# Attention with a routed expert layer on one core: the order of work on the engines made again with other costs of TensorE

## The chip, the cores and the metric

The kernel runs on one core of one Trainium2 chip. The metric is device time in microseconds (us), the median of several runs. The core has five engines that work side by side, each through its own instructions in a fixed order: TensorE (PE, matrix products; its loading of weights is shown apart, as PEld), VectorE (DVE), ScalarE (ACT), GpSimd (POOL), and SyncE (SP), which here issues transfers alone.

## The reference, cut to what matters

```python
# q, k, v: 8 batches x 8 heads x 576 positions x 64, float32
q_rot, k_rot = rotate(q), rotate(k)                      # rotary tables of 576 positions
scores = 1 / np.sqrt(64) * q_rot @ k_rot.transpose(0, 1, 3, 2)
attn = np.exp(scores - scores.max(-1, keepdims=True))
attn = attn / (attn.sum(-1, keepdims=True) + 1e-9)
x = (attn @ v).transpose(0, 2, 1, 3).reshape(8, 576, 512)
out = x.copy()
for b in range(8):
    s = x[b] @ w_gate
    top = np.argpartition(-s, 128)[:128]                 # 128 rows of the 576
    y = np.maximum(x[b, top] @ w1, 0) @ w2               # 512 -> 1024 -> 512
    out[b, top] = x[b, top] + y / (1 + np.exp(-s[top]))[:, None]
```

## The kernel before

The attention goes in 16 groups, g0 to g15, of four heads each (two groups make a batch). A group has two pairs of heads, c0 and c1. Pair number 2g + c of q and k is loaded by SP's transfers and multiplied with the rotary tables (`rotate`), nearly always on POOL: for q and for k a product of 128x1152 and a sum of 128x576, and for q a transfer `q_in<-q_in` behind them, which carries the result across partitions. Only the first pairs give some of these sums and products to DVE.

`units` is the product of 64 queries of a group with all 576 keys, for one pair or both: matmuls `banks<-k_in,q_in`, eight tiles of the array at a time (32 rows by 64 columns each; g0 uses four tiles of 64x64). `softmax` then takes the scores out of the PSUM banks in one of two ways, which the letters of `DRAINS` choose for each pair and block of queries:

- V: one DVE instruction, TENSOR_SCALAR_CACHE_REDUCE `prob<-banks`, scales, copies and finds the minimum.
- S: ACT copies (ACTIVATE `prob<-banks`), and DVE finds the minimum in a second instruction (TENSOR_REDUCE `nm<-prob`).

ACT then does the exponential (ACTIVATE `prob<-prob,nm`, 288 in all), and DVE transposes 32x32 blocks (`turn`). `value` is the product with v, again eight tiles (`banks<-prob,vt`, six parts of 48 matmuls a group); its result is copied (`ot<-banks`), transposed on PE (`banks<-ident,ot`) and scaled by ACT or DVE (`x<-banks,rs`). POOL multiplies the rows with the gate (`prod<-x,wg`), ACT or DVE adds them up, and each batch is routed: ranks, choice, an indirect load of 128 rows, the two products with w1 and w2 (whole-array matmuls), and an indirect store.

What stands in which order on each engine is decided nowhere in the loops. Each piece of work is recorded as an operation (`Order.op`), and `LINES` lists, engine by engine, the numbers of all operations in the order in which they are issued, two characters each. An operation that can go on two engines goes to the one in whose line it stands. `Order.run` walks through these lines with costs written in the code and gives out the PSUM banks by the times it gets; these costs are also those with which the lines were made. For PE it counts a change between kinds of tiles (`SWITCH`), a beginning after a wait, and a supply time: PE's instructions come in blocks of `BLOCK` = 256, and a block is not entered earlier than `FETCH` ns after the one before. Eight PSUM banks are shared: a pair's block of scores takes two, `value` takes banks 0 to 3, all other products one.

Of the kernel before, what the change touches and what calls it, by code (L numbers as in the profile page):

```python
# [33 lines left out]
fAhsfBfChxfDfEcyfNisfLfJiFizhHiMhIhJhKiRhLhMiXj7j1hRgbhThVcCcDkIkDgicFcGjdkOkZkUl3glcIcJcKcLjol9jpjqlejrjsjtlkmfjyjAjCgo
mrmEmlmylulvmLlwlxmQlylzmVm-lGlEgsgtopoBovk0lIgvgwoUoIoOo+k7gygzgAgBpap4nanbkancndnenfqdq6nonmkdnkplpmqqpnqkpoqCppqwpqkh
qInOpvpxpzkiqOshqUnVkkklsnstknkonYsykpkqr2sFr3sMr4r5sYr6r7sSn-rgrerct2tSu8tYu2o3o4o6rGueo7urultduxtetfuDtgthtirNo9tntrtp
oarQuRuSuTuUuVuWrTobv3v1u-ocrXverYr+vls1vor-s2s3vrs4vvvwvyvBvzvCvDvE""",
# [2 lines left out]
3N5i2a28263I3L3S5D3P2f5N5w5r5W5o5k5G5t5y5B5I5L5V5-5Y5m5q5S615Q41406X2h7647726-79492j7f6W744e7q717u4g7H6Z7h4i7D7b7s7A787k  # L40
7p7m7e7F7y7C7w6d6e7J7L6i95989c9f9m9j6m979o6r9q9h9e4V9a9u9l9z9H9s6t9L7Y7X9B9J9P9F9W9D9x829O4Z9UaOb29R8ba-8daXaU50b1b9b6bj
bdaQbbb8bhaWb4aZbsbnblaSbqa6a7bzbxbfd2bvd8bDdfdbbBaddhdldjdoafd6dddaakdsd4d08Ic+amdudndqdwdBaobPbQdzdGdKbY8HdEeEeRdJdMeK
eNeId+eVc3eXeMePeGf3eZeTe-f9f8f2dYdZc5fbfefge5f5e1fiflea8PgSfpgWecfkfngQftfrgVgYh0h7fHh4eecAhhhbhlg-hph2h9h6hjhfhuhohrhd
hwhzfGfFfOcziwhBitiGiJfTiCiyiviBiEiQfXiOiLiIiShNhOi+jaj2iWj0hShWiZiUkJh-jcj4j6i1j9cHjgkRl0i3jfkFjikHkNkWl4kLjwl8l2kYgqkQ
kTlbk-lfl6lhldljjvjulmmglojDgpmsmvmFmImmjImBjKmqmkmimomKmPmAmDmumxmHlBlAjMmYmSn0mNlHmXm+gumUoqoCoFlJoun2own4gxoXoJoRoHoE
lOoyoAoWosoQoZlQo-pdoNpcoTp7p3p1oLpfp9p6ngnhqeqhlSqaq7kennqjqtq9qcqvqlqgqpqDkfqzqsprqHqFqLpyqykjqPsiqnqKqTqRqNqBkmsopFqW
sqqYpHsksssCszsvrasmsxo1sGsJsEpJsBsNsIsLsPsZsRr9r8sTt1o0rhsVt3sXtTt7u9t5rms-tZrotVrqo5tXu3udubuiufo8u5usuot-u7uuu1uAuhuk
uwunuCuquHuztjtkuFtstxrVrUtzv2tBvtvA""",
# [2 lines left out]
323w3B3D3T3c3U3K3O5l3R5K3H5j5M5C5A5x5v5H5F3V435s5U5+605X5R5P635p6462666V6Y6545737d706g7o7j7a7l7r7x7g7K7I7v774F7M4I7E4J4L
4K4M7B7O4O7P6k7Q7N969n4R9g9k9t7+999d9r9y9w4W9X9K9I9Y9E9C9N9V4U9T846v9Q809ZaR899-9+8sb0aP8z8y8v8x8waVbmb7a9bgbab3aYbrbpbe
bkbFbwbubEbCc-cZd58BabbHbAdcdidgbIbGdmd98EbSdp55d3dOdvdtdNdAdydPdFdDdIbUbWdLeHc1dQdReU8MeLeOeFe+eYeSd-f1fuf78Jfvfaf4fdff
ckgRgPcne3cpcrcocqfwfjctfmfsgUg+gXfqfxfyhCcw8UcBhkh8fIhehch1hnh5hihqhthvhDhyhAhEhFfMfKhGiAiuhQixiKiPiDiHfViNjjiVjkiTiYi-
j8gajbgfghgegdj3gghUj5cEkMjlgjkKkGkEjekPk+kVl1gmjhl7jmkSjnl5kXjxcMlplalcgrlqlglilrlllnmjjzjBltlsmpmtmwmzmJmnmhmGmOmMmCn5
mRmTn6j-mWn3lDlFmZn1n7otn8k5k3k4oGozk6k2oDoVnjoMoxoPp2oSk8oroKn9oYpggCpbp5k9p0p8pekbpipkpjphqiqfnlnpq8qbnupuqrquqonwqmny
qGqZkgqAqxnNpsqEqJnUnSpwpAnQnRnTqMqSqQslqVqXnWq+r0spsusrsjswq-sDnZr1krrbsAt8sKo2sQsHsOt9t0s+tasWsUrfrdt6t4tWuctUu0uatctb
u6rFt+uIrMrIrLrJu4rKujuvtmumutuLuguyupuKuBuEuJuGuNuOrOuPuMuQtotqrRuYrWu+uXv4v9v0v6v7v8v5vdodvgvkvivhvjrZvmvnvps0vsvxs5vu
vF""",
# [1 line left out]
0z0E0A0B0H2L2M2N2O2I2J2G2H575859235e5a5f5c5d2e6R426S6M6N6P2g6K6L6Q6f2i8Y4d8Z4f914h8W8X924H8-904PaK7Z6qaL4S6saFaGaIaD6uaJ
aE888a8ca8cV8ucWcQcRcTcUcOcP8CeAbRevajeweyaleBezan8Feteu56c0c2gLgEgMgGgHgFgJgKc4cme9ebcuiiedijipiqcxikiliniofShPkAfUkBfW
8Vkvkwkykzktkugch+i0i2gkmcgnmdmam7m8mbm5m6lCjHohjJcNoiomonofjLokogolq1lNp+niq3lPq4p-k1pYgDpZkcq2lRs9saptsentnvnxsfscs7sd
nPs8pEnXtIpGtPtJtQtKkspIn+tNtOtLrlrnrptlrHrPuZrStwtytAvfoevqs6vG""",
# [3 lines left out]
at8raqapcXcS6o6naCcccdcac9aAc8cb85ayaz87c6ceexaB86c7cheCcfagemelefegeiehcgekb-cjciejgNgIahenesaib+bZg5eoe7fZg2fYf+erg3f-
g1e6e8epeqirg0g4imiai8ibg8idg6g7g9i7i4i6i9fQkCfPi5iekxifihjVicfRhZhXjTjRjUjOjShYjQjNjPjWmeigm9jYjXlWlZlVj+l+lXjZlUlTlYm2
ojl-jGoojFnDnEnznBnFnCm1m4nGjEnHlLnInAm3lMlKm0q0pMq5pNpQpPpRnKnJpKpLpTnMpOnLpSpXpUpWnspVsbsgrznqrArsryrrrxrunrpDrtrvrwtR  # L70
pCrDtMrErCripBtCrBrjtErktGtHtFtDvctuttvavbtv""",
}


# [240 lines left out]
def attention_moe_kernel(ctx: ExitStack, tc: tile.TileContext, q, k, v, w_gate, w1, w2, rope, halves, outs, cap):  # L315
# [156 lines left out]
    DRAINS = (
        ("SVVSVVSSS", "SSSVSSSVS"),
        ("SSSVVSVSS", "SSSSSVVSS"),
        ("SSVVVVVVV", "VSVVVVVSV"),
        ("VSSVVVSSS", "SSSSVSVSV"),
        ("SSSSVSSVV", "SSSVVVVSV"),
        ("SSSSSSVVS", "VSSSVVVVV"),
        ("VSSSSSVVV", "VVSVSVVVS"),
        ("SSSSVVVSS", "VSVVSSVSV"),  # L480
        ("VVVSSSVVV", "VSSSVVSVV"),
        ("SVSVSVSVV", "SSSVVSVSS"),
        ("VSVVVSVSV", "VVSVSVVVV"),
        ("SSSVSVVVS", "VVSSSVVSV"),
        ("SSSSVVSVV", "VVSVSSVSS"),
        ("SSSVVSVSV", "SSVSSVSVV"),
        ("SSVSSSSSS", "VVVSSVVVV"),
        ("SSSSSVSVV", "VVVVSSVSV"),
    )
# [630 lines left out]
```

## Time and profile before

| | |
|---|---|
| median of 3 runs | 511.87 us (511.4 to 513.64) |
| the profiled execution | 514.22 us, of it 512.5 us in the span of its records |
| PE busy | 481.9 us, 10148 matmuls and as many weight loads |
| DVE busy | 448.5 us |
| ACT busy | 393.4 us |
| POOL busy | 351.0 us |
| moved by DMA | 86.86 MB, mean 169 GB/s |

Busy time is the sum of the instructions of an engine over the whole span. The start differs from the rest: in the first 125 us PE is busy for 107 us, and from 125 us to 446 us for 313.9 of 321 us.

### The profile page before, as it was taken

To read this page: it belongs to the slowest core of one execution; us is meant where nothing else is said; L and a number is where in the kernel's file an instruction comes from. 1 tells how busy PE (TensorE), PEld (TensorE's weight loads), DVE (VectorE), ACT (ScalarE), POOL (GpSimd) and SP (SyncE) were. 2 spreads that over 40 slices of the span, in tenths; PEclk is the share of its full clock that TensorE was granted. 3 is DMA by queue.
4 is the path that set the end of the run, shared out by engine and by line. 5 is a ranking of instruction groups with operands and counts; after the bars stand their busy time and mean duration, and the time that the engine had idled before them with its cause. 6 is when DMAs were issued, how large, how long until landed. Compare 5 with 4: busy or idle time off the path is not lost.

```text
span 512.5 us, 23466 instructions
## 1 busy us (share of the span) xinstructions
PE 481.9 (94%) x10148; PEld 343.0 (67%) x10148; DVE 448.5 (88%) x783; ACT 393.4 (77%) x1065; POOL 351.0 (68%) x316
## 2 busy tenths in 40 slices
...
GB/s 286 287 228 256 200 206 181 228 172 199 220 194 155 179 180 222 157 183 195 187 208 134 184 153 185 161 229 141 214 138 186 190 103 128 24 86 23 114 22 41
DMA packets 52488, 86.86 MB, mean 169 GB/s; under 512 B 5920, under 2 KB 29216, under 8 KB 52384
## 3 DMA queue, kind: packets, MB, share of 16 engines
...
q8 instruction: 80, 1.31, 1.1%
q10 hardware_dynamic: 544, 0.59, 0.4%
q14 instruction: 24, 0.20, 0.1%
...
## 4 chain that ended last, share of the span: by engine, by line
PE 71%; ACT 8%; POOL 8%; issue 6%; DMA 3%; DVE 3%; SPq 0%; POOLq 0%; DVEq 0%
PE banks L241 71%; ACT prob L241 5%; POOL k_in L241 4%; POOL q_in L241 3%; DMA q_in<-q_dram 2%; ACT ot L241 2%; DVE prob L241 2%; ACT x L241 1%; POOL prod L241 1%; DMA k_in<-k_dram 1%; ACT prod L241 0%; SPq L241 0%; POOL out_dram L241 0%; DVE q_in L241 0%; POOLq L1115 0%
## 5 line engine op out<-in xcount | busy, mean ns | idle before, releaser
L241 ACT ACTIVATE prob<-prob,nm 128x576 f32<-128x576 f32 x288 | 220.7, 774 | 20.3 <-DVE prob L241 14.1
L241 PE MATMUL banks<-k_in,q_in 32*64 32x288 f32 (+1 forms) x4464 | 191.0, 415 | 19.8 <-ACT prob L241 6.2
L241 DVE STREAM_TRANSPOSE prob<-prob 128x2304 f32<-128x2304 f32 (+2 forms) x98 | 186.5, 1923 | 0.5 <-ACT prob L241 0.3
L241 PE MATMUL banks<-prob,vt 32*64 32x288 f32 x4608 | 163.3, 404 | 1.8 <-issue 0.6
L241 PEld LDWEIGHTS banks<-k_in,q_in 32*64 32x64 f32 (+1 forms) x4464 | 109.1, 133 | 79.7 <-ACT prob L241 19.1
L241 PEld LDWEIGHTS banks<-prob,vt 32*64 32x64 f32 x4608 | 120.7, 132 | 33.2 <-issue 7.6
L241 DVE TENSOR_SCALAR_CACHE_REDUCE prob<-banks 128x576 f32<-128x576 f32 x140 | 102.8, 748 | 19.3 <-PE banks L241 18.0
L241 ACT ACTIVATE prob<-banks 128x576 f32<-128x576 f32 x148 | 93.1, 652 | 29.8 <-PE banks L241 29.3
L241 DVE TENSOR_REDUCE nm<-prob 128x1 f32<-128x576 f32 x148 | 105.7, 737 | 1.1 <-ACT prob L241 1.0
L241 POOL TENSOR_TENSOR prod<-x,wg 128x512 f32<-128x512 f32 (+1 forms) x45 | 49.5, 1100 | 56.6 <-ACT prod L241 16.6
L241 POOL TENSOR_TENSOR q_in<-q_in,tabk 128x1152 f32<-128x1152 f32 (+1 forms) x31 | 80.5, 2597 | 7.6 <-DMA q_in<-q_dram 5.4
L241 POOL TENSOR_TENSOR k_in<-k_in,tabh 128x1152 f32<-128x1152 f32 x30 | 79.6, 2657 | 5.5 <-DMA k_in<-k_dram 3.5
L241 PEld LDWEIGHTS banks<-xt,w1t 128*128 128x128 f32 x512 | 58.9, 192 | 4.1 <-issue 3.6
L241 PE MATMUL banks<-xt,w1t 128*128 128x128 f32 x512 | 61.2, 277 | 0.0
L241 PE MATMUL banks<-w2t,ht 128*128 128x512 f32 x128 | 58.5, 599 | 0.0
L241 ACT ACTIVATION_READ_ACCUMULATOR prob<-prob,nm 128x1 f32 x288 | 57.3, 199 | 0.0
L241 POOL TENSOR_TENSOR q_in<-q_in 128x576 f32<-128x576 f32 (+2 forms) x33 | 45.2, 1371 | 10.4 <-DVE q_in L241 9.2
L241 POOL TENSOR_TENSOR k_in<-k_in 128x576 f32<-128x576 f32 x31 | 43.8, 1417 | 2.7 <-DVE k_in L241 1.4
L241 PEld LDWEIGHTS banks<-w2t,ht 128*128 128x128 f32 x128 | 23.0, 190 | 24.4 <-issue 22.9
L241 POOL TENSOR_SCALAR sel<-slots,rank 128x128 bf16<-128x128 bf16 x30 | 17.7, 604 | 26.8 <-DVE rank L241 26.8
L241 ACT ACTIVATE x<-banks,rs 128x64 f32<-128x64 f32 (+1 forms) x144 | 31.2, 322 | 4.5 <-PE banks L241 3.3
L241 ACT ACTIVATE prod<-prod 128x256 f32<-128x256 f32 (+1 forms) x63 | 25.8, 414 | 9.1 <-POOL prod L241 9.1
...
## 6 DMA issues: line engine op xcount, KB each, us to landing
...
```

The source lines that it names most:

```text
L241: i = made(*args, **kwargs)
```

## The change

Two costs of TensorE are raised, and the tables that follow from them are made again. After a wait the beginning of an operation of eight tiles counts 130 ns instead of 70 (the other two kinds stay at 70), and the supply time of a block of instructions counts 3950 ns instead of 3600. `LINES` (all five engines) and `DRAINS` are new. Every operation of the reference is computed as before; no tile, pool or transfer is added or removed.

```diff
-BLOCK, FETCH = 256, 3600.0
+BLOCK, FETCH = 256, 3950.0
+
+
+RESTART = (70.0, 130.0, 70.0)
...
     "PE": """
-010T1r101i190J1H1v1A0O141N0X1e1m3d2V333o2Q3i2+381X3u1Y1Z3A1+1-3F203M5h29275J255z5u5E5T5n5Z5O3W3X3Y3Z3+3-6U7546446+487c7n
+010T1i1q10190J1m0O1z1G0X1M1u1d143a302S3k3f352O2X1V3r1W3y1X1Y3E1Z1+3K5e27235G255w5B5p5k5S5Y5M3T3U3V3W3X3Y6T7441436Z457b7n
...
-                            begin += SWITCH[mode][o.mode] + 70.0 * (t > free[e] + 1)
+                            begin += SWITCH[mode][o.mode] + RESTART[o.mode] * (t > free[e] + 1)
...
     DRAINS = (
-        ("SVVSVVSSS", "SSSVSSSVS"),
-        ("SSSVVSVSS", "SSSSSVVSS"),
-        ("SSVVVVVVV", "VSVVVVVSV"),
+        ("SVVVVVSSV", "SSSSVSSVS"),
+        ("VSSVSSVSV", "SSSVSSSVS"),
+        ("SVSVVSSVV", "VVSVVVVSV"),
```

The letters V in `DRAINS`, group by group from g0: before 6, 5, 14, 7, 8, 8, 10, 8, 11, 8, 13, 7, 9, 8, 8, 10 (140 of 288); now 8, 6, 12, 6, 10, 6, 11, 7, 9, 6, 11, 7, 9, 7, 9, 10 (134).

Of the operations that can go to two engines, the scaling of rows (`x<-banks,rs`) stands in ACT's line 24 times before and 20 now (DVE 24 and 28), adding up the gate's products 38 and 34 times (DVE 7 and 11), the relu of the expert layer (`ht<-banks`) 11 and 15 times (DVE 5 and 1). PE's line has 394 operations before and now, of the same kinds.

The rows below are instructions in the order in which they stand on an engine, equal ones that follow each other in one row. The first place is ACT in g0 and at the beginning of g1, before and then now: `prob_87<-banks` is an S copy of g0, `prob_88<-banks` one of g1, `prob_87,sums_92<-prob_87,nm_94` an exponential of g0.

```order
L241 ACTIVATE prob_87<-banks 128x576
L241 ACTIVATE prob_87,sums_92<-prob_87,nm_94 128x576
L241 ACTIVATE prob_87<-banks 128x576 x4
L241 ACTIVATE prob_87,sums_92<-prob_87,nm_94 128x576
L241 ACTIVATE prob_87<-banks 128x576 x2
L241 ACTIVATE prob_87,sums_92<-prob_87,nm_94 128x576 x3
L241 ACTIVATE prob_87<-banks 128x576
L241 ACTIVATE prob_87,sums_92<-prob_87,nm_94 128x576 x2
L241 ACTIVATE prob_87<-banks 128x576
L241 ACTIVATE prob_87,sums_92<-prob_87,nm_94 128x576 x5
L241 ACTIVATE prob_88<-banks 128x576
L241 ACTIVATE prob_87,sums_92<-prob_87,nm_94 128x576
```

```order
L244 ACTIVATE prob_87<-banks 128x576 x4
L244 ACTIVATE prob_87,sums_92<-prob_87,nm_94 128x576 x4
L244 ACTIVATE prob_87<-banks 128x576 x3
L244 ACTIVATE prob_87,sums_92<-prob_87,nm_94 128x576
L244 ACTIVATE prob_87<-banks 128x576
L244 ACTIVATE prob_87,sums_92<-prob_87,nm_94 128x576 x3
L244 ACTIVATE prob_87<-banks 128x576
L244 ACTIVATE prob_87,sums_92<-prob_87,nm_94 128x576 x5
L244 ACTIVATE prob_88<-banks 128x576 x5
L244 ACTIVATE prob_88,sums_93<-prob_88,nm_95 128x576
```

g0 has two S copies fewer, and the first five copies of g1 now stand together behind the last exponential of g0.

The second place is DVE in g0, behind its first products of the rotation, before and then now: TENSOR_SCALAR `prob_87,nm_94<-banks` is a V, `q_in_75` and `q_in_76` are the queries of the first two pairs.

```order
L241 TENSOR_SCALAR prob_87,nm_94<-banks 128x576 x3
L241 TENSOR_TENSOR q_in_76<-q_in_76,tabk 128x576
L241 STREAM_TRANSPOSE prob_87<-prob_87 128x576 x2
L241 TENSOR_REDUCE nm_94<-prob_87 128x1
L241 STREAM_TRANSPOSE prob_87<-prob_87 128x576
```

```order
L244 TENSOR_SCALAR prob_87,nm_94<-banks 128x576 x3
L244 TENSOR_TENSOR q_in_76<-q_in_76,tabk 128x576
L244 TENSOR_TENSOR q_in_75<-q_in_75 128x192
L244 STREAM_TRANSPOSE prob_87<-prob_87 128x576
L244 TENSOR_SCALAR prob_87,nm_94<-banks 128x576
```

A sum of 192 columns that stood on POOL stands on DVE now, ahead of the first transpose.

The third place is ACT where g1 ends and g2 has its scores taken out, before and then now: `prob_87<-banks` is an S copy of g2 here, `x_90<-banks,rs_96` the scaling of g0's rows.

```order
L241 ACTIVATE x_90<-banks,rs_96 64x64 x4
L241 ACTIVATE x_90<-banks,rs_96 128x64 x16
L241 ACTIVATE prob_88,sums_93<-prob_88,nm_95 128x576 x3
L241 ACTIVATE prob_87,sums_92<-prob_87,nm_94 128x576
L241 ACTIVATE prob_88,sums_93<-prob_88,nm_95 128x576
L241 ACTIVATE prod_98,gp_99<-prod_98 128x256 x2
L241 ACTIVATE prob_87,sums_92<-prob_87,nm_94 128x576 x2
L241 ACTIVATE prob_87<-banks 128x576 x3
L241 ACTIVATE prob_87,sums_92<-prob_87,nm_94 128x576 x15
```

```order
L244 ACTIVATE x_90<-banks,rs_96 128x64 x8
L244 ACTIVATE prob_87<-banks 128x576
L244 ACTIVATE x_90<-banks,rs_96 128x64 x8
L244 ACTIVATE prob_88,sums_93<-prob_88,nm_95 128x576 x3
L244 ACTIVATE prob_87,sums_92<-prob_87,nm_94 128x576
L244 ACTIVATE prob_87<-banks 128x576 x2
L244 ACTIVATE prob_87,sums_92<-prob_87,nm_94 128x576 x2
L244 ACTIVATE prob_87<-banks 128x576
L244 ACTIVATE prod_98,gp_99<-prod_98 128x256 x2
L244 ACTIVATE prob_87,sums_92<-prob_87,nm_94 128x576 x4
L244 ACTIVATE prob_87<-banks 128x576
L244 ACTIVATE prob_87,sums_92<-prob_87,nm_94 128x576 x11
```

g2's S copies are six instead of four, and they stand between the scalings and exponentials rather than in one piece.

## Rows read from the trace of the kernel before

**Rows 1.** Page, busy time of each engine and its share of the span.

```profile
PE 481.9 (94%) x10148; PEld 343.0 (67%) x10148; DVE 448.5 (88%) x783; ACT 393.4 (77%) x1065; POOL 351.0 (68%) x316
```

**Rows 2.** Windows: length, then busy time of each engine, PE's granted clock, DMA.

```profile
0.00:36.00 36.00, 26.61 (x220) 16.54 (x220) 30.92 (x63) 21.59 (x49) 22.56 (x25) 1.00 0.82 266
36.00:60.00 24.00, 23.39 (x598) 17.20 (x606) 23.22 (x36) 20.78 (x49) 17.27 (x13) 0.93 0.78 234
60.00:97.00 37.00, 31.39 (x810) 18.70 (x794) 35.05 (x59) 35.78 (x112) 29.22 (x24) 0.95 0.68 197
97.00:125.00 28.00, 25.54 (x713) 19.18 (x721) 27.28 (x46) 27.14 (x76) 26.01 (x27) 1.00 0.67 201
125.00:446.00 321.00, 313.87 (x6942) 226.11 (x6925) 300.11 (x504) 269.49 (x728) 242.29 (x207) 1.00 0.59 172
446.00:512.50 66.50, 61.14 (x905) 45.22 (x889) 31.96 (x80) 18.64 (x57) 13.69 (x23) 0.99 0.18 55
```

**Rows 3.** Windows, four short stretches of the start, same columns.

```profile
28.00:36.00 8.00, 2.63 (x32) 1.16 (x32) 8.00 (x12) 8.00 (x22) 7.84 (x4) 1.00 0.68 189
36.00:40.00 4.00, 4.00 (x56) 2.33 (x60) 3.68 (x6) 2.23 (x5) 3.92 (x3) 0.58 0.92 287
...
60.00:70.50 10.50, 7.44 (x188) 3.70 (x172) 10.10 (x22) 10.50 (x39) 6.66 (x8) 1.00 0.69 211
70.50:74.50 4.00, 3.86 (x72) 2.37 (x80) 2.90 (x8) 4.00 (x11) 3.92 (x3) 0.57 0.64 153
```

**Rows 4.** Timeline of PE: start, length, matmuls; in brackets PE's idle time before.

```profile
31.70 1.91 PE L241 MATMUL banks<-k_in,q_in 32*64 32x288 f32 x24 [2.95 <-DMA q_in<-q_in]
36.00 7.47 PE L241 MATMUL banks<-k_in,q_in 32*64 32x288 f32 x121 [2.39 <-ACT prob L241]
...
66.54 2.58 PE L241 MATMUL banks<-k_in,q_in 32*64 32x288 f32 x64 [0.33 <-DVE prob L241]
70.64 3.89 PE L241 MATMUL banks<-k_in,q_in 32*64 32x288 f32 x64 [1.52 <-ACT prob L241]
```

**Rows 5.** Chain that ended last, its longest piece: start, length.

```profile
446.40 50.41 PE banks L241 x841
```

**Rows 6.** Groups of ACT: count, busy us, mean ns of one.

```profile
L241 ACT ACTIVATE prob<-banks 128x576 f32<-128x576 f32 x148 | 93.1, 652 | 29.8 <-PE banks L241 29.3
L241 ACT ACTIVATE x<-banks,rs 128x64 f32<-128x64 f32 (+1 forms) x144 | 31.2, 322 | 4.5 <-PE banks L241 3.3 <-POOL sel L241 1.2
L241 ACT ACTIVATE prod<-prod 128x256 f32<-128x256 f32 (+1 forms) x63 | 25.8, 414 | 9.1 <-POOL prod L241 9.1
L241 ACT ACTIVATE ht<-banks 128x512 f32<-128x512 f32 x11 | 6.6, 604 | 16.9 <-PE banks L241 16.8
```

**Rows 7.** Groups of DVE, same columns.

```profile
L241 DVE TENSOR_REDUCE nm<-prob 128x1 f32<-128x576 f32 x148 | 105.7, 737 | 1.1 <-ACT prob L241 1.0
L241 DVE TENSOR_SCALAR_CACHE_REDUCE prob<-banks 128x576 f32<-128x576 f32 x140 | 102.8, 748 | 19.3 <-PE banks L241 18.0 <-ACT prob L241 0.3
L241 DVE TENSOR_TENSOR x<-banks,rs 128x512 f32<-128x512 f32 (+1 forms) x24 | 14.7, 634 | 1.4 <-PE banks L241 1.4
L241 DVE TENSOR_REDUCE gp<-prod 128x2 f32<-128x512 f32 (+1 forms) x7 | 4.2, 606 | 1.1 <-POOL prod L241 1.1
L241 DVE TENSOR_TENSOR k_in<-k_in 128x288 f32<-128x288 f32 x2 | 0.9, 458 | 0.1
```

**Rows 8.** Waits from 125 to 446 us: total, times, longest.

```profile
PEld banks L241 <- ACT prob L241: 16.1, 35, 1.3
```

**Rows 9.** Timeline: weight loads behind a gap; two long runs of eight-tile matmuls.

```profile
47.84 1.21 PEld L241 LDWEIGHTS banks<-prob,vt 32*64 32x64 f32 x48 [0.71 <-issue]
...
307.19 0.91 PEld L241 LDWEIGHTS banks<-prob,vt 32*64 32x64 f32 x33 [0.75 <-issue]
...
452.73 4.60 PE L241 MATMUL banks<-prob,vt 32*64 32x288 f32 x144
```

**Rows 10.** Page, the DMA queue that brings PE's instructions: packets, MB, share.

```profile
q8 instruction: 80, 1.31, 1.1%
```

More of the change, by code (lines that the diff above doesn't have):

```diff
@@ L34 @@
[L34 to L37, printed above, removed]
-    "ACT": """
-0203121t0K0V1a1k1I0M1w1c1B0P151E1K1O0Y1D1M1y1n0R1Q1R1G171T1p1g3e0+2W343r2R3g3l3q2-392T2Y3v363k313n3b3t3z3x3C3E3G3J21223Q
@@ L40 @@
[L40 to L48, printed above, removed]
-    "DVE": """
-0s0t0w0x0u0v0G0y0U0D0C1s111j0F131u0L0W1b1l1L0N1J1d1x0Q161C1F1P1f0Z1V1o0S1z1S1U1W181q1h2X353f3p3s0-3j3m2S3h303a3y2Z372U24
@@ L51 @@
[L51 to L59, printed above, removed]
+010T1i1q10190J1m0O1z1G0X1M1u1d143a302S3k3f352O2X1V3r1W3y1X1Y3E1Z1+3K5e27235G255w5B5p5k5S5Y5M3T3U3V3W3X3Y6T7441436Z457b7n
+7h7u7G7A6667684D696a6b4K6g6i9b949i6k4N7R9o7S9u7T7U9F7V7W9z9K9Q4Q7-81834U4VaLaYaR4X4Y8tb3bgba9+bm9-a0a1bsa2a3bycYd28Aa8df
@@ new lines @@
+d84+aaac8D4-50dl51bJdrbKbLbMdwbNbOdBdGbVbXbT8GeCePeI8K8LdReWdSf0dTdUf6dVdWfcgOe1cld-e38Nfh8OcsfogTgZh38Qcv8R8S8Thghafzhm
+fAhsfBhyfCfDfEcyfNiufLfJiHiBhJiOhKiUhLhMhNhOi+jaj5hVhXhTgbcCcDkHkNcFgicGjhl8kTkZl2glcIcJcKcLjslejtjujvlkjwjxlqmljCjEjGgo
+mxmJmrmElAlBlCmQlDmXlElFn1n6lMlKgsgtovoHoBlOk4gvgwo+oOoUp4kbgygzgAgBpgpangkenhninjnknlqcqjnsnunqkhprqwpsqqptqKpuqDpvpwkl
+nUpBqQkmpFn-pDqVsoq-kokpsvsBkro2kssHktkur9sOrasVrbrct3rdres+rnrlrjo5t8tYufu9u2o9oaocrNuloduyustjuEtktltmuJtntorUoftttxog
+rXtvuXuYuZu+u-v0r+ohv5v7v9s2oivks5s3vrs8vus6s9savxsbvEvBvCvFvHvIvJvK""",
+    "ACT": """
@@ new lines @@
+02030V1s0K1k120M0P1A1D1H1C1F0R1J1v0Y1e1L151O1g1b1P0+171R1o1x3b312T3o3l3d36332V2Y2Q3j3v3s3h3n3q3B3x382+3u3A3D3F1-203N3J5f
+28245H263P3M3H5A5t5q5h5D5V2d5F5y5J5L5N5m5j5s5o5+5v5P5R5U605X3Z3+6W2f787544716+2h6Y7e7o4b7r7i7q4d7v7H704f6V737x7B7m7a7k7z
+7g7t7L7D7d7F6c6d7J776h9c9f95989l6l9a9h9p9k4S979e6q9r9t9n6s9y9J7X7Y9A9w9N9E9H9C9U9M824W9SaMb09PaS8baV8daZaQ4ZaOb7b4bhblbd
+aUb6b9a-b2brbnbfaXbtbcbjbpa5a4bzcZd3bBdgd9bxbDdcbvd1abdkaddodbd7dedid5aic-dndvakdqdtdyamdAbPbQ8IdJdFdD8HeDeTdLdIeMdZeJeQ
+8MeHeLeVeXeOeFf3c3eSe-eZf7f9dYdXf5c5fbf2e0e4fefgflfigS8PfkfpgWfnfte9gVgYgQh0frebh7edg-h4cAhhhbh9hdhphlh2h6hthohjhrhBhfhv
@@ new lines @@
+hxhAfFfGfOcziyhDiviIiLiChRiRiGixiEiTiAiNiViQiKhPhQi-j2fXjbjej1hUj4cEkIiZiXi3kOjgj9cHjdjkl9kWj7jjl5k-i5jml1kMkSkKgqkQlbkY
+l4lhldkVl7lnlgljlmjyjzlplsmmlujHgpmymBmNmKmsjMmqlImumomwmAmUmRmGmDjOmImPm+lGlHmTmMmWlNn5mZn0gun3owoIoLlPoAnan8oCgxp1oPoV
+lUp0oEoyoGoKlWoXp3p9p5pjpboRoZpfp7oToNplpipdkjnnnmqdqgqkqnkiqAqxqmnAqtqpqfqNqiqCqHqEnEqJpyqsqzqPqMqvknpGqUqWssspq+pLqSqY
+kqsrswr1sEr3qGrhpNsLsAsIsDsysKo7susGsSsPsNsZsXsUsRt7rgrfrot5o6t9t0tZrtugt2tdu3rvu6tbucuirxobu1t-u5umupuboeukuzuvuxu8ueuo
+uBuuuruGuDuNuLtptquItuv3s0v2tFr-tHv6s4vzs7vG""",
+    "DVE": """
@@ new lines @@
+0s0t0w0x0u0v0G0y0U0D0C1j1r110F0B0W1a0L1t1n130N0Q1B1E1I1K1N1S0S1l1f1w160Z1T1Q1h0-1c1U1p18323c221y3i3g2U372P343m3p3e3w2W3t
+3z2R2Z3C3Q3I3R3O3G5i393L2-5K5I5g5z5x5C5E3S5n5l5r5T5-405Z5u5W5Q5O636162656U64466X42767c6f796-7p7l7f727y7K7s7j7w4C7I7M7E4J
+4G4I4H7C4F7O4L7P6j7Q7N994O9j9g969s9q9m9d9x9v9V9G9I4T7+9W9D9B9L9T4R9R809X846u9OaP899Z9Y8saNa+8y8z8w8x8vaTbkbibbb5a7b8beb1
+bqaWbFbobwbubEbCbAd0c+d68Ba9d4bGdhdjdabHbIdm8EbSdddp52dNdudsdMdxdzdOdCdEdHbWbYbUdKeGc18JdPdQeEeNeKeUe+eYeRf1fud+f4faf8fv
+fffdckgPgRcqe2cpcrcncofwfjctfmfsgUg+fqgXfxcwhEfy8Uhkh8hecBhch1hnh5hihqhwfIhFhuhzhGhHhCfMfKhIiFiwiDhSfTiPiziSiJfViMiYjnjo
@@ new lines @@
+iWgaj0j8j6hYgfj3hWgeggghgdjci1jfkJkLjpgjkRkPjilckUk+l3jll0jqkXgmjrlacMl6grlvlflwjBlilllxlolrltmpjDjFlylzmvmtmnmCmLmFmHmz
+mOnblJmVmYmSncn4n2n7n9m-lLndjQozk3nekak8k6k9oFoJk7oMo-oSoDoxoYnfoWp8oQp2kcpmgCphnpkdp6pepopkkfpcpnpqppntnrnvlYqeqhqoqlqB
+qyqrqLqOnCpAr4qInTkkqFpxqunXn+nZnWqRnYpCqTpEo0qZr5r0qXr2sqr7sCszstsxo3r6r8sJsFkvrisMtesTsQsYsWtft4t6tgt1o8s-rmrkpPtctau0
+ujt+uauhthu4tirMudu7rQrTuOrRrPrSuquCutuwuRuntsuAuPuHuFuTuQuMuKuSrVuWuUuVtwv4tyrYtDs1v1v8vdvavevfvcvbvjojvqvmvnvpvovsvtvv
+vyvDvAscvL""",
@@ L60 @@
     "POOL": """
[L61 to L64, printed above, removed]
+0z0E0A0H2J2K2L2M2G2H2E2F21545659575b5c555a6Q3-6R2c6L2e6O6M6J6P6K8Y2g8Z6e4a4c4e91928W8X8-907Z4M4EaI4P6paD6raJaE6taGaBaCaH
```

43 lines of the change are left out of this document (22 added, 21 removed).

## The prediction, made before the changed kernel ran

> **What bounds the kernel now.** I read the page's busy times first. PE is busy for 481.9 of 512.5 us [rows 1], so what an order can win lies in the 30.6 us in which PE has nothing running, or in stretches in which PE runs slower than it could. The windows show where these are [rows 2]. The reader is to take PE's busy time from the length of each window. Up to 125 us PE lacks 9.4, 0.6, 5.6 and 2.5 us, together 18.1. From 125 to 446 us it lacks 7.1 of 321 us. From 446 us to the end it lacks 5.4, and the chain that ended last has one unbroken piece of PE there, 50.41 us [rows 5], so the end follows PE to the us, and a us won earlier is won at the end.
>
> What holds PE back early is seen in the same windows: from 60 to 125 us DVE is busy for 62.3 of 65 us and ACT for 62.9. The short windows sharpen that [rows 3]. From 28 to 36 us ACT and DVE are both busy for 8.00 of 8.00 us while PE works for 2.63; from 60 to 70.5 us ACT has no idle time at all and DVE 0.4 us. These are the softmax of g0, and of g1 and g2. The timeline names the waits of PE there [rows 4]: 2.95 us for the transfer `q_in<-q_in`, 2.39 us and 1.52 us for ACT.
>
> Behind two of these waits the granted clock falls: it is 0.58 and 0.57 of full speed from 36 to 40 us and from 70.5 to 74.5 us [rows 3], a mix of 2.4 GHz and its lower level of 1.2 GHz. What that costs is read in one pair of rows [rows 4]: 64 matmuls of eight tiles take 2.58 us at full speed and 3.89 us there, 1.3 us more. In the long middle ACT is busy for 84% and DVE for 93.5% [rows 2], and PE alone is the bound.
>
> **PE's own work: 0.** The matmuls are the same, so only the neighbours of each can change. I counted neighbouring operations of PE's line in five classes (products of scores with eight tiles, and in g0 with four; products with v; all whole-array work as one class). A score product is followed by another 82 times before and 82 now, by a product with v 40 and 40 times; a product with v by a score product 42 and 42 times. Whole-array work is entered from tiles 38 times in both, and left 38 times. So the changes of tile kind and the alternation cost the same, and no class of neighbours pays or saves. This is the main reason why I expect little.
>
> **The two raised costs: 0.** They are numbers in the walk, not instructions. That a beginning behind a wait is dear is not doubted, but no beginning is taken away by counting it. For the supply time, the trace shows single gaps: weight loads start 0.71 and 0.75 us late with nothing named as the cause in the midst of a product with v [rows 9]. But 144 matmuls of one kind also run through in 4.60 us [rows 9], more than one block of 256 instructions (a matmul and its load are two), with no gap shown. Instructions come as 80 packets, 1.31 MB [rows 10], in both orders. If eight more or eight fewer of these 80 block changes met such a gap, that would be 8 x 0.73 less what PE still had queued; PE itself idled for a part only, so I bound the term at plus and minus 3 us and take 0, since the counts of neighbours are equal.
>
> The Trainium skill, "Runtime: NRT & Kernel Launch", section "Instruction fetch mechanics", says that the sequencer fetches blocks of 256 instructions ahead by itself and that crossing a block is mostly hidden. The trace agrees with the size (16 KB a packet), and differs at places, by 0.7 us each. By that rule alone this term would be 0 as well, with no bounds around it.
>
> **Work moved among ACT, DVE and POOL, up to 125 us.** A letter changed from V to S adds 0.652 us to ACT [rows 6], and leaves DVE where it was: 0.748 becomes 0.737 us [rows 7]. Place by place:
> - g0, seen at 28 to 36 us: two S fewer, ACT -1.3 us. DVE gains at most 0.46 us by the sum of 192 columns (the nearest row is a sum of 288 columns, 0.458 [rows 7]), and POOL loses it. Both were full, so I take half of ACT's relief, -0.6. The 2.95 us wait in this stretch stays: the transfer and the sums of the second group's queries ahead of it stand as before behind the reload of a table that DVE's product of `q_in_76` releases, and that product keeps its place.
> - g1 and g2, at 60 to 75 us: two S more in g2, ACT +1.3 us where it has no idle time. An S copy lets a bank go without DVE, so not all of it delays PE: half, +0.6. (g1's one S fewer falls at 36 to 60 us, where ACT has 3.2 us idle, and is worth nothing.)
> - 75 to 97 us: one scaling of two blocks of rows goes from ACT to DVE, 8 x 0.322 = 2.6 us off ACT and 0.63 on DVE [rows 6, 7]; g3 has one S more, +0.65. ACT -1.9, DVE +0.6, both over 94% busy [rows 2]. A third of ACT's relief: -0.6.
> - g4, 97 to 125 us: two S fewer, ACT -1.3, PE lacks 2.5 us there. A third: -0.4.
>
> The sum is -1.0 us. Its bounds: all of ACT's relief (1.3 + 1.9 + 1.3 = 4.5) counts and the +1.3 does not, -4.5; or no relief counts and g2's +1.3 and DVE's 0.46 + 0.63 count in full, +2.4. The shares of a half and a third are my choice, near the middle, since where ACT and DVE are both full neither alone decides.
>
> **From 125 us on.** ACT: eight S more, 8 x 0.652 = +5.2; three scalings fewer, 3 x 2.6 = -7.7; four sums of two or fewer blocks fewer, 4 x 2 x 0.414 = -3.3; four relus more, 4 x 0.604 = +2.4 [rows 6]; together -3.4 us of 269.5. DVE: three scalings, +1.9, four sums, +2.4 [rows 7], four relus fewer, about -2.4 if as long as ACT's; together +1.9 of 300. PE's weight loads wait for ACT's softmax for 16.1 of the 321 us [rows 8], 5%, so 3.4 us less are worth -0.2. Nothing here hides from PE: it is covered because PE is the bound, and if that cover went, DVE's +1.9 would count. Bounds: half of the 7.1 us that PE lacks is won, -3.5, or DVE's +1.9.
>
> In the last 66 us PE's whole-array work keeps its order but for single neighbours; the last part of the product with w1 now stands ahead of the first part of the one with w2 instead of behind it, and neither waits for the other. 0.
>
> **The sum.** -1.0 - 0.2 = -1.2 us. The profiled execution took 514.22 us, 512.5 in the span and 1.7 around it, which nothing here touches; it would take 513.0. The profiled execution lies 2.35 us above the median of 511.87 (0.6 above the slowest of the three runs), and I apply the same sum to the median: **510.7 us**.
>
> **Rivals.** 0.5% is 2.56 us, about what a measurement of this kernel can tell from no change: 509.3 and 514.4 are the limits.
> - *The change does nothing* (511.9). The costs are numbers, PE's neighbours are equal in count, and ACT and DVE hold each other. Against it: some twenty pieces do move between engines that are full early.
> - *ACT was what held the start* (faster). For it: two of the three long waits of PE name ACT, and the first five copies of g1 now stand together, so banks come free one behind the other. The relief counts nearly in full (-3.9) and the wait at 70.6 us gets so short that the clock stays up there (-1.3): 511.87 - 5.2 = 506.7. Against it: DVE was as full as ACT.
> - *The middle gives* (faster). The waits of PE in 321 us shrink by a third, 2.4 us, beside the -1.2: 508.3. For it: -3.4 us on ACT. Against it: DVE, at 93.5%, gets more.
> - *A third drop of the clock* (slower). g2's six S copies lie between the scalings and exponentials, in the stretch in which ACT has no idle time. If the exponentials behind them, and with them DVE's transposes, come late enough for PE to wait a second time as it does at 36 us, that is 1.9 us more of waiting (the 1.3 and half of DVE's 1.1) and 1.3 us for the matmuls behind it at the lower clock: 511.87 + 3.2 = 515.1. It decides where a new wait of PE of over 1.3 us stands between 60 and 100 us with the clock below 1 behind it.
> - *More block changes in long runs of tiles* (slower), as bounded above: up to 514.9.
>
> **How the numbers follow.** The forecast of 510.7 gets 0.30, no effect at all 0.12: together 0.42 for within 0.5%. ACT at the start gets 0.23 and the middle 0.15: 0.38 for faster. The drop of the clock gets 0.13 and the block changes 0.07: 0.20 for slower. The forecast's own range is 509.3 to 512.6. To hold 8 in 10 the range goes to 506.0, which takes in both faster cases but for their far ends, and up to 514.5, which leaves out most of the slower cases.
>
> **What would show it.** PE's busy time in the window from 125 us on should stay within 2 us of 313.9 for as much work, the chain should end in PE alone again, and the 1.2 us should lie before 125 us: g1's second wait of 2.39 us shorter, g2's waits at 62 to 72 us not. Should the first half gain more than 3 us, I under-counted ACT; should PE's idle time between 125 and 446 us change by more than 2 us either way, the equal counts of neighbours were no guide. The forecast is wrong altogether if a stretch with a lowered clock appears or goes.

## The result, and the profile of the changed kernel

The changed kernel takes **514.53 us** (median of 20 runs, 512.21 to 517.31), the kernel before 511.65 us beside it (20 runs, 509.72 to 513.64). The ratio is 1.0061, 95% interval 1.0045 to 1.0078: slower by 2.9 us, where 510.7 was forecast.

The profiled execution took 515.57 us, 513.7 in the span. Busy times, and the windows that answer to [rows 2] (length, then PE, PEld, DVE, ACT, POOL, PE's granted clock, DMA):

```profile
PE 482.9 (94%) x10148; PEld 337.5 (66%) x10148; DVE 447.1 (87%) x781; ACT 394.7 (77%) x1048; POOL 349.2 (68%) x311
```

```profile
0.00:36.00 36.00, 28.32 (x224) 17.75 (x228) 31.22 (x66) 21.72 (x49) 22.46 (x26) 0.94 0.83 276
36.00:60.00 24.00, 23.59 (x582) 17.12 (x579) 20.95 (x33) 19.59 (x46) 16.76 (x11) 0.88 0.74 213
60.00:97.00 37.00, 30.44 (x833) 18.50 (x840) 36.91 (x62) 36.49 (x111) 29.25 (x25) 1.00 0.71 210
97.00:125.00 28.00, 24.58 (x679) 17.50 (x671) 25.68 (x43) 25.00 (x71) 23.67 (x24) 1.00 0.76 230
125.00:446.00 321.00, 313.93 (x6959) 222.86 (x6951) 302.13 (x503) 271.47 (x717) 244.35 (x209) 1.00 0.57 167
446.00:513.70 67.70, 62.03 (x913) 43.77 (x895) 30.18 (x79) 20.43 (x62) 12.70 (x19) 0.99 0.18 57
```

Take PE from each length, as with [rows 2]: up to 125 us it lacks 7.7, 0.4, 6.6 and 3.4 us, together 18.1, exactly as much as before; from 125 to 446 us 7.1, as before. By these sums nothing happened. The early waits (PE's timeline, against [rows 4]) have changed places: the second one of g1 is 1.11 us instead of 2.39, and the 1.52 us at 70 us have become 0.83 and 0.69.

```profile
30.87 3.83 PE L244 MATMUL banks<-k_in,q_in 32*64 32x288 f32 x24 [2.66 <-DMA q_in<-q_in]
35.81 8.59 PE L244 MATMUL banks<-k_in,q_in 32*64 32x288 f32 x121 [1.11 <-ACT prob L244]
...
70.63 1.23 PE L244 MATMUL banks<-k_in,q_in 32*64 32x288 f32 x32 [0.83 <-ACT prob L244]
72.56 1.23 PE L244 MATMUL banks<-k_in,q_in 32*64 32x288 f32 x32 [0.69 <-DVE prob L244]
```

The clock differs too: one stretch at 0.50 from 31.5 to 41.7 us, and 1.00 where [rows 3] has 0.57 (windows of the changed kernel).

```profile
31.50:41.70 10.20, 9.09 (x110) 5.85 (x112) 7.43 (x12) 7.10 (x16) 9.71 (x8) 0.50 0.76 215
70.50:74.50 4.00, 2.92 (x80) 1.63 (x88) 4.00 (x11) 4.00 (x14) 4.00 (x3) 1.00 0.81 227
```

But this pair of profiles cannot explain the loss. The profiled execution of before is a long one of its kind (514.22 us against a median of 511.65), so the pair is 1.35 us apart where the medians are 2.9; and the mean clock of single runs of the changed kernel goes from 0.984 to 0.997. So more executions were profiled, on other chips too. On most of these the kernel before takes 508 us, so each kernel is compared with before on its own chip.

### The profile page after: what moved, and what is told of

It is laid out like the page before. It is cut to its first block, busy times and chain, and to the rows that moved or that the text cites. A ratio compares the mean times of both kernels' runs of the same rounds, so it can differ in the third digit from the quotient of the medians.

```text
span 513.7 us, 23429 instructions
## 1 busy us (share of the span) xinstructions
PE 482.9 (94%) x10148; PEld 337.5 (66%) x10148; DVE 447.1 (87%) x781; ACT 394.7 (77%) x1048; POOL 349.2 (68%) x311
## 4 chain that ended last, share of the span: by engine, by line
PE 67%; ACT 14%; DMA 7%; issue 6%; DVE 4%; POOL 1%; SPq 1%; POOLq 0%; DVEq 0%
PE banks L244 67%; ACT prob L244 10%; DVE prob L244 2%; DMA q_in<-q_dram 2%; ACT ot L244 2%; DMA k_in<-k_dram 2%; DMA vt<-v_dram 1%; DMA out_dram<-x 1%; ACT x L244 1%; DVE nm L244 1%; ACT prod L244 1%; DMA w1t<-w_dram 1%; DMA q_in<-q_in 1%; SPq L244 1%; DVE q_in L244 0%
## 5 line engine op out<-in xcount | busy, mean ns | idle before, releaser
L244 PE MATMUL banks<-k_in,q_in 32*64 32x288 f32 (+1 forms) x4464 | 187.2, 416 | 19.0 <-ACT prob L244 6.1
L244 PE MATMUL banks<-prob,vt 32*64 32x288 f32 x4608 | 160.4, 403 | 2.4 <-issue 1.0
L244 PEld LDWEIGHTS banks<-k_in,q_in 32*64 32x64 f32 (+1 forms) x4464 | 106.3, 133 | 82.2 <-ACT prob L244 25.0
L244 PEld LDWEIGHTS banks<-prob,vt 32*64 32x64 f32 x4608 | 114.2, 132 | 37.9 <-issue 9.0
L244 ACT ACTIVATE prob<-banks 128x576 f32<-128x576 f32 x154 | 96.6, 651 | 32.6 <-PE banks L244 31.8
L244 DVE TENSOR_SCALAR_CACHE_REDUCE prob<-banks 128x576 f32<-128x576 f32 x134 | 98.3, 747 | 17.8 <-PE banks L244 14.8
L244 DVE TENSOR_REDUCE nm<-prob 128x1 f32<-128x576 f32 x154 | 109.1, 736 | 0.5 <-ACT prob L244 0.5
L244 POOL TENSOR_TENSOR q_in<-q_in 128x576 f32<-128x576 f32 (+1 forms) x32 | 44.7, 1399 | 10.3 <-DVE q_in L244 9.0
L244 ACT COPY ot<-banks 128x576 f32<-128x576 f32 x30 | 17.7, 640 | 17.6 <-PE banks L244 16.8
L244 ACT ACTIVATE x<-banks,rs 128x64 f32<-128x64 f32 (+1 forms) x124 | 27.0, 324 | 2.8 <-PE banks L244 2.3
```

What stands on the lines that cost most here:

```text
L244: i = made(*args, **kwargs)
```

## The experiments

All were timed in five rounds, 11 or 12 runs each against 29 to 35 of the kernel before. The ratio is the one on record, which is not the quotient of the two medians: the quotient lies up to 0.3% away (new_gather_early 1.0057, old_to_125_gather_early 1.0032, new_gather_early_2 1.0013). A difference of 0.2% between two rows therefore says little.

| kernel | median, before | ratio (95%) |
|---|---|---|
| old_again | 508.39, 507.98 | 1.0006 (0.9984 to 1.0028) |
| new_again | 510.13, 507.98 | 1.0053 (1.0020 to 1.0087) |
| new_order_old_costs | 511.55, 508.25 | 1.0052 (1.0031 to 1.0073) |
| new_gather_early | 514.42, 511.52 | 1.0027 (1.0004 to 1.0051) |
| new_gather_early_2 | 508.52, 507.86 | 1.0003 (0.9976 to 1.0031) |
| new_gather_and_casts | 512.96, 511.52 | 1.0024 (0.9997 to 1.0052) |
| old_gather_late | 514.21, 511.52 | 1.0050 (1.0023 to 1.0077) |
| old_to_125 | 512.63, 508.25 | 1.0078 (1.0052 to 1.0104) |
| old_to_125_gather_early | 509.51, 507.86 | 1.0012 (0.9986 to 1.0037) |
| old_order_new_costs | 511.32, 508.25 | 1.0047 (1.0022 to 1.0072) |
| old_order_new_costs_2 | 510.52, 508.08 | 1.0051 (1.0025 to 1.0076) |
| new_to_125 | 510.44, 508.25 | 1.0053 (1.0022 to 1.0085) |
| new_to_125_casts | 511.04, 507.86 | 1.0053 (1.0022 to 1.0085) |
| new_to_125_old_costs | 507.53, 508.08 | 0.9996 (0.9966 to 1.0026) |
| old_other_banks | 508.27, 507.98 | 1.0004 (0.9977 to 1.0032) |
| old_half_block | 509.62, 507.98 | 1.0045 (1.0013 to 1.0077) |
| new_gather_half_block | 510.02, 507.86 | 1.0051 (1.0021 to 1.0081) |
| old_whole_block | 508.64, 508.08 | 1.0021 (0.9996 to 1.0046) |

### Numbers or order, start or rest?

The order is exchanged in whole (`LINES`, `DRAINS`), or in part: new_to_125 has the changed order for the operations that the walk starts before 125 us and the old one behind them, old_to_125 the reverse, and both keep the raised numbers. The numbers are exchanged as here:

```diff
-BLOCK, FETCH = 256, 3950.0
+BLOCK, FETCH = 256, 3600.0
-RESTART = (70.0, 130.0, 70.0)
+RESTART = (70.0, 70.0, 70.0)
```

**old_order_new_costs.** 

> The order and the letters of before with the two raised numbers. No engine's line changes; what changes is which banks of PSUM an operation gets, for 299 of 850 bank uses, since the walk hands a bank out by its own times, and the order in which the engines' instructions are written. Theory A (the loss of 2.9 us lies in the order of the lines): within 1 us of before, ratio 1.000. Rival B (the banks that the raised numbers hand out cost it): most of the loss, ratio 1.004 to 1.007.

**new_order_old_costs.** 

> The order and the letters of the changed kernel with the two old numbers (9 of 850 bank uses differ from the changed kernel). Theory A: as the changed kernel, ratio to before 1.006. Rival B: if the numbers alone did harm it comes back to 1.000 to 1.002; with 9 bank uses only I expect no more than 0.5 us from it.

**new_to_125.** 

> The changed order for all operations that the walk starts before 125 us, the order of before for the rest, raised numbers. Theory E (the loss is made early: the clock is low for 10 us at a stretch, and GpSimd waits for 21.6 instead of 5.4 us for transfers of queries): all of the loss, ratio 1.005 to 1.007. Rival M (it is made from 125 us on, in single stalls of PE of 0.5 to 2 us): ratio 0.999 to 1.002.

**old_to_125.** 

> The mirror: the order of before for all operations that the walk starts before 125 us, the changed order for the rest, raised numbers. Theory E: ratio 0.999 to 1.001. Rival M: ratio 1.005 to 1.007. If both halves show some of it (1.002 to 1.004 each) the loss is spread and neither theory holds by itself.

All four came out slower by about half a per cent or more, which fits no theory: either half of the order cost something, and so did the numbers alone. Rival B held for the old order (1.0047), and not for the new one (1.0052 with the old numbers). So the comparison itself was tried next.

**old_again** (no edit). 

> The kernel before itself, unchanged, timed against itself: what the comparison gives for no change at all. Theory A (orders and bank hand-outs really differ by half a per cent): ratio 1.000, interval within 0.3% of it. Rival N (a program built anew is measured some tenths of a per cent above the one that it is compared with, so that all four variants so far came out at 1.005): ratio 1.003 to 1.005.

**new_again** (no edit). 

> The changed kernel itself once more, on this chip. Theory A: ratio 1.004 to 1.008 as before. Rival N: about the ratio of the unchanged kernel against itself plus 0 to 0.3%.

No change gives 1.0006, and the changed kernel 1.0053 again: the comparison is sound, and rival N falls.

### The gather of the third batch

new_again was profiled in an execution of 509.56 us, old_again in one of 506.21. Where their PE timelines part is plain (the views here and below are cut at 243 and 258 us, so a row at an edge can show a part of its matmuls). new_again:

```profile
242.61 2.89 PE L244 MATMUL banks<-prob,vt 32*64 32x288 f32 x88
248.75 0.63 PE L244 MATMUL banks<-ident,xe 128*128 128x128 f32 x4 [3.25 <-DMA xe<-out_dram,idx]
...
249.61 2.22 PE L244 MATMUL banks<-k_in,q_in 32*64 32x288 f32 x32
251.76 1.57 PE L244 MATMUL banks<-ident,ot 128*128 128x128 f32 x8
...
255.84 1.72 PE L244 MATMUL banks<-prob,vt 32*64 32x288 f32 x48 [0.21 <-ACT prob L244]
```

old_again:

```profile
242.62 3.11 PE L241 MATMUL banks<-prob,vt 32*64 32x288 f32 x95
245.66 0.66 PE L241 MATMUL banks<-ident,xe 128*128 128x128 f32 x4
...
247.40 1.23 PE L241 MATMUL banks<-k_in,q_in 32*64 32x288 f32 x32
248.55 1.09 PE L241 MATMUL banks<-ident,ot 128*128 128x128 f32 x8
...
252.16 1.72 PE L241 MATMUL banks<-prob,vt 32*64 32x288 f32 x48
```

From the end of g7's product with v (245.50 and 245.73) to the next product with v it is 10.34 us in the new order and 6.43 in the old: 3.9 us. Up to there the two executions are level, and their spans end 3.3 us apart (507.7 and 504.4), so in this pair the place accounts for the whole difference. PE waits 3.25 us for `xe`, the rows that batch 2's experts work on, and behind the wait the same 32 matmuls take 2.22 us instead of 1.23 and the 8 transposes 1.57 instead of 1.09. That is the clock (windows of new_again):

```profile
247.00:251.00 4.00, 2.25 (x30) 1.48 (x38) 2.27 (x2) 1.29 (x5) 1.90 (x2) 0.80 0.68 230
251.00:255.00 4.00, 4.00 (x80) 2.49 (x72) 2.03 (x3) 2.43 (x6) 4.00 (x3) 0.77 0.40 130
```

POOL issues that gather. old_again, then new_again:

```profile
233.65 1.41 POOL L241 TENSOR_TENSOR q_in<-q_in 128x576 f32<-128x576 f32 x1
235.01 0.19 POOL L241 CAST idx<-gg 128x1 uint32<-128x1 f32 x1
235.48 1.12 POOL L241 DMA_INDIRECT xe<-out_dram,idx  x1 [0.28 <-POOL idx L241]
```

```profile
234.64 2.66 POOL L244 TENSOR_TENSOR q_in<-q_in,tabk 128x1152 f32<-128x1152 f32 x1
237.38 1.42 POOL L244 TENSOR_TENSOR q_in<-q_in 128x576 f32<-128x576 f32 x1
238.75 2.69 POOL L244 TENSOR_TENSOR k_in<-k_in,tabh 128x1152 f32<-128x1152 f32 x1
241.36 0.21 POOL L244 CAST idx<-gg 128x1 uint32<-128x1 f32 x1
241.85 1.13 POOL L244 DMA_INDIRECT xe<-out_dram,idx  x1 [0.28 <-POOL idx L244]
```

The new order puts three rotations more ahead of it, 6.4 us, though the index was ready on DVE at 227.7 us. The gather also lands more slowly there, 6.8 us after its issue against 4.5. In the new order the indirect store of the batch before (`out_dram<-xe,idx`) is issued 1.4 us behind it, in the old 24 us behind. In the four profiles with the store so close the gather takes 5.6 to 6.8 us, in the other sixteen 3.6 to 5.6; whether the store is the cause is not shown, and old_gather_late below has the wait without it.

In the profile of the changed kernel shown first the wait is missing, and so this was not seen there: the gather stands just as late (issued at 246.02, landed 5.6 us later), but PE came to it at 251.6 us by itself, since the 144 matmuls of the product ahead took 6.50 us instead of the 4.60 of [rows 9], with weight loads late by 0.56, 0.53 and 0.54 us (no cause named).

The test moves that one operation (cx in POOL's line) across the three rotations (im, in, ip), in the new order forward, and in the old one back by as many, without touching a bank:

```diff
-...ecisikiminipcx8V...
+...ecisikcximinip8V...
```

**new_gather_early.** 

> The changed kernel with one step moved on GpSimd alone: the gather of the rows of the third batch (cast of the index, indirect transfer out_dram to xe) goes in front of the three steps of rotation (q_in, q_in, k_in; 2.7 + 1.4 + 2.7 us) that the changed order puts ahead of it; bank hand-out unchanged in all uses. Theory G (most of the loss is that gather: it lands after PE has come to its transposes, PE waits 2.4 to 3.3 us at about 249 us, and the clock can fall behind it): no wait of PE for xe, and the ratio to before comes down from 1.005 to 0.998 to 1.002. Rival (the loss is spread over many small places, and this wait is covered later): 1.003 to 1.006 with the wait gone.

**new_gather_early_2** (the same). 

> The changed order with the early gather once more, since its ratio (1.0027, from 1.0004 to 1.0051) lies between the two theories. Theory G (the gather is most of the loss): 0.999 to 1.002. Theory F (without the wait at 249 us, PE's instruction supply falls behind at 256 to 266 us: two block changes there came 2.6 and 1.2 us late, where the changed kernel, having just waited, has none): 1.002 to 1.004, with gaps of together over 2 us at 258 to 266 us again.

**old_gather_late.** 

> The kernel before with the mirror of it: the same gather three steps of rotation (2.7 + 1.4 + 2.7 us) later on GpSimd, all banks and all other orders kept. Theory G: PE waits 2 to 3 us for xe at about 247 us and the ratio is 1.003 to 1.007. Rival: 1.000 to 1.002.

In the new order with the early gather (new_gather_early_2), and in the old one with the late gather, PE's timeline reads:

```profile
242.65 4.59 PE L244 MATMUL banks<-prob,vt 32*64 32x288 f32 x144
247.17 0.66 PE L244 MATMUL banks<-ident,xe 128*128 128x128 f32 x4
...
253.65 1.72 PE L244 MATMUL banks<-prob,vt 32*64 32x288 f32 x48
```

```profile
244.15 3.65 PE L246 MATMUL banks<-prob,vt 32*64 32x288 f32 x96
250.53 0.63 PE L246 MATMUL banks<-ident,xe 128*128 128x128 f32 x4 [2.73 <-DMA xe<-out_dram,idx]
...
251.30 2.22 PE L246 MATMUL banks<-k_in,q_in 32*64 32x288 f32 x32
...
257.65 0.74 PE L246 MATMUL banks<-prob,vt 32*64 32x288 f32 x16 [0.21 <-ACT prob L246]
```

The stretch is 6.41 us long in the one and 9.85 in the other: the wait follows the gather, whichever order surrounds it. The slow clock follows the wait in three of four profiles; in old_to_125, behind 2.63 us of waiting, the clock stays at 1.00 and the 32 matmuls take 1.23 us. The old order with nothing but this gather late is as slow as the changed kernel (1.0050). The new order with it early is at 1.0003 on one chip and 1.0027 on another, where old_gather_late was timed too and the two medians are equal (514.42 and 514.21). So the late gather is shown to cost half a per cent in the old order, and moving it early wins that back on the one chip and about half of it on the other. The changed kernel itself was timed beside neither. The profile of new_gather_early shows what theory F means, weight loads late by 2.48 and 1.06 us where new_gather_early_2 and new_again have none over 0.41:

```profile
261.06 0.94 PEld L244 LDWEIGHTS banks<-prob,vt 32*64 32x64 f32 x37 [2.48 <-issue]
...
265.75 2.38 PEld L244 LDWEIGHTS banks<-prob,vt 32*64 32x64 f32 x82 [1.06 <-issue]
```

Counted in the twenty traces, all 44 loads that come 0.7 us late or more within a product with v stand at the same place of the 256 instructions of a block, the 193rd or 194th, so they are changes of block. But theory F does not hold: new_gather_and_casts has them at the same two places (0.70 and 1.61 us), and so have new_order_old_costs (1.37 and 1.34) and old_to_125 (1.25 and 1.32), in which PE has waited for the gather. What makes them late in one execution and not in another stays open. The repeat fell in theory G's range.

**old_to_125_gather_early.** 

> The old order up to 125 us, the changed one behind it (1.0078 as it was), with the gather early as in the other kernel. Theory G: 0.5 to 0.7% less than without, 1.001 to 1.003. If the rest of the loss were made before 125 us: 0.999 to 1.001. Rival (spread): 1.005 to 1.007.

1.0078 becomes 1.0012 (on another chip), as theory G has it, though the interval takes in 1.000 too. A smaller wait of the same kind, 1.0 us at 115 us for the casts `tok`, was to be taken away by exchanging two neighbours on POOL:

```diff
-8Y2g8Z6e4a4c4e91928W8X8-907Z4M4E...
+8Y2g8Z6e4a4c4e91928W8X8-907Z4E4M...
```

**new_gather_and_casts.** 

> As the kernel with the early gather, and in the first batch the casts of the scores (tok) stand again in front of the selection on GpSimd, so that PE need not wait 1.0 us for them at about 115 us. Theory G with the small wait counted: 1 us below the early gather alone or covered, so ratio 0.996 to 1.001. Rival: 1.002 to 1.005.

1.0024 against 1.0027 on the same chip: nothing that these intervals can tell. The exchange could win little: the wait for `tok` goes, but PE now waits twice for `sel` in its place, 0.8 us together.

### What the raised numbers do to the old order

**old_order_new_costs_2** (the same again). 

> The old order with the raised numbers (1.0047 on another chip) once more. Theory B: 1.003 to 1.006. Rival (the first value was partly the clock of that chip's runs, 0.9902 in the mean against 0.9918): 0.999 to 1.002.

**new_to_125_casts** (the exchange above). 

> The changed order up to 125 us, the old one behind it (1.0053 as it was), with the casts of the first batch in front of the selection, which should take away PE's wait of 1.0 us for tok. If that wait is what the start loses: 1.001 to 1.003. Rival (the start's loss has to do with the clock, which in the slower third of that kernel's runs was lower): 1.004 to 1.006 and again a few runs 3 us above the rest.

**new_to_125_old_costs** (numbers as above). 

> The changed order up to 125 us, the old order behind it, with the two old numbers: behind 186 us none of 533 bank uses differs from the kernel before (102 differ with the raised numbers, which gave 1.0053). Theory B (where the old order stays, the raised numbers cost it by the banks that they hand out): 0.999 to 1.002. Rival E (the changed start itself costs half a per cent): 1.004 to 1.006.

Theory B holds: 1.0051 once more, and with the old numbers the changed start costs nothing (0.9996). new_to_125_casts stays at 1.0053, but decides nothing, since its profile too has 0.8 us of waits for `sel` in place of the one for `tok`. All four profiles of the old rest with raised numbers have one wait in common, 1.3 us for DVE ahead of g7's product with v; none with the old numbers has it. old_order_new_costs_2, then new_to_125_old_costs:

```profile
231.71 2.35 PE L244 MATMUL banks<-k_in,q_in 32*64 32x288 f32 x64
235.33 1.72 PE L244 MATMUL banks<-prob,vt 32*64 32x288 f32 x48 [1.27 <-DVE prob L244]
```

```profile
231.10 2.45 PE L244 MATMUL banks<-k_in,q_in 32*64 32x288 f32 x64
233.31 1.71 PE L244 MATMUL banks<-prob,vt 32*64 32x288 f32 x48
```

The walk, with other times, hands out other banks; the product needs banks 0 to 3 and here waits for a DVE instruction that, I take it, still reads one of them. That the banks are the cause is argued and not tested: the raised numbers also change the order in which the instructions are written, and nothing separates the two. The wait is 1.3 of the 2.4 to 2.7 us; the rest is not explained. Which bank is named does not matter:

```diff
-key=lambda x: (..., self.clear(x, kind), x)
+key=lambda x: (..., self.clear(x, kind), -x)
```

**old_other_banks.** 

> The old order, letters and numbers; where several banks are equally long free the walk takes the last and not the first, so 722 bank uses name another bank and nothing else moves (the walk gives the same times and engines). Theory C (the kernel before is a fortunate draw, and any new layout of the same work costs about 0.5%): 1.003 to 1.006. Rival (which bank does not matter; what matters is how long a use waits for its bank): 0.998 to 1.002.

1.0004, as the rival has it. Theory C, that any new layout costs half a per cent, falls.

### Where blocks of instructions change

The opening matmuls, which feed nothing, are divided otherwise (whole block: 4 and 82):

```diff
-        for _ in range(22):
-            nc.tensor.matmul(bank_of(warm)[:, 0:P], ident, ident, start=True, stop=True)
+        for n in [P] * 12 + [16] * 42:
+            nc.tensor.matmul(bank_of(warm)[0:n, 0:n], ident[:, 0:n], ident[:, 0:n], start=True, stop=True)
```

**old_half_block.** 

> The old order, with TensorE's opening matmuls made as 12 of 128 columns and 42 of 16 columns in place of 22 of 128 (they feed nothing): 128 instructions more, so each of the later changes of instruction block falls half a block of 256 away from where it was. Theory C: 1.003 to 1.006, and other places of PE with a gap of over 0.4 us. Rival (block changes cost the same wherever they fall, some 3 us above the even pace in all): 0.998 to 1.002, give or take up to 1 us of the opening's own length.

**new_gather_half_block.** 

> The changed order with the early gather, and TensorE's opening as 12 matmuls of 128 columns and 42 of 16 in place of 22 of 128, so that block changes fall half a block of 256 instructions away. Theory F: the two late block changes at 256 to 266 us go or become shorter, and the ratio falls below the early gather alone, by 1 to 2.5 us, to 0.998 to 1.001. Rival (a half block more costs what it cost the old order, 1.0045): 1.004 to 1.007.

**old_whole_block.** 

> The old order, TensorE's opening as 4 matmuls of 128 columns and 82 of 16: 256 instructions more than before, so every later block change falls where it fell before, behind an opening of small matmuls that by the half-block kernel's rates (0.166 and 0.0375 us for each of two passes) lasts about 7.5 us, as it did. Phase theory (the half block cost 0.45% because block changes fell elsewhere): 0.999 to 1.002. Rival (the opening of small matmuls costs it): 1.004 or more.

Half a block costs either order 0.5%, a whole one 0.2%, with an interval that touches both theories. Theory F's 0.998 to 1.001 for new_gather_half_block is missed (1.0051), although its profile has no load over 0.33 us late without a named cause between 254 and 270 us. The 1.0045 of old_half_block is what theory C gave, though that theory fell above. The opening is no longer than before (7.15, 7.73 and 6.34 us against 7.32 in the profile of before and 7.88 in old_again). So where the changes fall matters probably, but it is not settled: the small matmuls at the start may have a share.

## Why the prediction was wrong

**The step that failed** is "From 125 us on" (-0.2). It counted what moves on ACT and DVE and looked at POOL only up to 125 us. On POOL one gather moves behind three rotations, 6.4 us, and its reader on PE, which had 5.7 us to spare (old_again: issue at 235.48, landing 4.5 us later, first use at 245.66), waits 2.4 to 3.3 us. In new_again 0.7 us of the 3.25 is the slack overrun and 2.3 us the slower landing, which no count of instructions would have shown. "Nothing here hides from PE" was the sentence: work that PE waits for only when it is late is hidden until it is moved past its slack. Wait and clock are 3.9 us at the place; old_gather_late's ratio says 2.6 us at the end. How much of the first 2.9 us the gather makes on its own chip is not shown: the profile there lacks the wait, and on the other chip with 511.5 us before, 0.2 to 0.3% stay with the gather early.

**What bounds the kernel**: right. PE is busy for 313.93 us of the middle, as 313.87 before. But the prediction's own sign, a change of PE's idle time there by more than 2 us, does appear in the second pair: of the 321 us PE lacks 9.1 in new_again and 6.8 in old_again.

**PE's own work, 0**: not contradicted; new_gather_early_2 has the new order of all matmuls at 1.0003, and 1.0027 on the other chip is left without a cause.

**The two raised costs, 0**: right for this change (the new order with the old numbers 1.0052), for a wrong reason. They are no instructions, but they decide banks and the order of writing, and on the old order they cost 0.5%. The bound of 3 us either way had a good premise: its two gaps of 0.7 us [rows 9] are changes of block by the count above.

**Moves up to 125 us, -1.0**: too much. PE lacks 18.1 us in both profiles. Up to 60 us the changed kernel won 1.9 us (g1's second wait did get shorter, as forecast), and from 60 to 125 us it gave them back, 1.0 of it in the new wait for `tok`. The changed start with the old rest and the old numbers is at 0.9996.

**The rivals.** The third drop of the clock had the mechanism and nearly the price (1.9 us of waiting and 1.3 of clock; measured 3.25 and, from the rows, 0.99 + 0.48), but sat at 60 to 100 us behind ACT, and had 0.13. Block changes: the changed kernel's ratio does not need them, since the late gather alone gives 1.0050. What stays with the gather early on the other chip may be theirs (2.48 and 1.06 us in that profile); that is not shown.

**What would show it.** The forecast was to be "wrong altogether if a stretch with a lowered clock appears or goes": no good sign for early stretches, since they come and go between executions of one program. old_again, which is the kernel before, has this window where [rows 3] has 0.57:

```profile
70.50:74.50 4.00, 3.67 (x121) 2.43 (x112) 4.00 (x10) 4.00 (x11) 3.92 (x3) 1.00 0.74 224
```

The Trainium skill, "Runtime: NRT & Kernel Launch", section "Instruction fetch mechanics", calls the crossing of a block mostly hidden. These runs agree at some crossings ([rows 9]: 144 matmuls and their loads, more than a block, in 4.60 us without a gap) and differ at others: up to 2.48 us late in one profile, and 0.5% more time where all crossings are shifted by half a block.
